# A decode step of attention and MLP on one core: wo's rows per partition, w1 in two transfers, w2's blocks in another order

## The chip, the core and the metric

The kernel runs on one core of a Trainium2 chip. A core has a matrix engine (TensorE, PE in the profile, with its weight loads listed as PEld), a vector engine (VectorE, DVE), a scalar engine for activations (ScalarE, ACT), GpSimd (POOL) and a sequencer that issues transfers (SyncE, SP). Sixteen DMA engines move data between the main memory (HBM) and the on-chip memory SBUF, which has 128 partitions. Matmuls write to another memory, PSUM. The metric is the time of one execution on the device in microseconds, lower is better; several executions are made and the median is given.

## What is computed

One token for each of four sequences (B = 4) goes through one transformer block: an attention over a cache of 4096 positions with 32 heads of 128, and an MLP with 1728 hidden units. The model's width is 640. Everything is bf16 in memory.

```python
def _A_ref(x, k_cache, v_cache, wq, wo):       # x: (4, 1, 640)
    q = (x @ wq).reshape(B, Sq, 32, 128).transpose(0, 2, 1, 3)
    scores = einsum("bhqd,bhkd->bhqk", q, k_cache) * (128 ** -0.5)
    p = softmax(scores)
    o = einsum("bhqk,bhkd->bhqd", p, v_cache)
    return o.transpose(0, 2, 1, 3).reshape(B, Sq, 32 * 128) @ wo

def _B_ref(x, w1, b1, w2):
    h = x @ w1 + b1
    act = h * tanh(log1p(exp(-abs(h))) + where(h > 0, h, 0))
    return act @ w2

h  = x + _A_ref(layernorm(x), k_cache, v_cache, wq, wo)
h2 = h + _B_ref(layernorm(h), w1, b1, w2)
```

The two caches are 134 MB each. wq and wo are 5.2 MB each, w1 and w2 2.2 MB each.

## The kernel before

**Work units.** The caches are cut into NG = 32 groups: group g is one sequence b = g % 4 and one set hq = g // 4 of four heads (G = 4). A K block of a group has the tile `kt`, [128, R = 128, 128]: a head takes 32 partitions, and a partition holds 128 positions in a row, 32 KB. V is held in the same way in `vt`. There are two buffers for each of them (KBUFS, VBUFS), and one transfer of 4096 KB loads one block. The last K block comes in two transfers, the last V block in four (L95 to L98).

**A group's steps** (loop from L408). `mul_and_sum` (L339) multiplies a K block in place by the broadcast q on DVE (L348), in four pieces, and PE sums the products over the head dimension with matmuls against the identity (L355). `finish_sum` (L364) reduces the rest on DVE. `softmax(g - 1)` (L374) finds the maximum by a PE transpose and forms the exponentials on ACT, with their sums. `pv_moving(g - 1)` (L252) multiplies the probabilities with V on PE, `pv_copy` takes the result out of PSUM on ACT, and `add_blocks(g - 2)` (L267) sums it into the o of four sequences. When a set of four groups is done, `row_sums` and `normalise` (L292, L304) divide by the sums of the exponentials and write `otn[:, hq]` in bf16: a partition is one of the 128 head dimensions, and the columns are sequence and head.

**The output projection** `project(hq)` (L325) adds the four heads of a set into the PSUM tile `yT` with 20 matmuls: weights are 128 x 128 pieces of `wo_sb`, the moving side is `otn` with four columns. It runs after `pv_moving` of the steps in `PROJ_AT` (L224): g = 14 to 17 for sets 0 to 3, g = 22, 26, 30 for sets 4 to 6. The last set is projected behind the loop (L499).

**Order of instructions.** The program is written out by hand (L75): each engine runs its instructions in the order of the code, and semaphores hold one back until its operands are there. All loads but x's are issued by SP in code order: at the end of step g, K block g + 2, then V block g + 1, then (steps 8 to 11, `WO_AT`) a quarter of wo, eight heads (L447). In step 8 the 3.4 KB row b1 follows (L452). The transfers of SP's queue are carried out in this order too, by all 16 DMA engines, and an issue waits on SP until its buffer is free.

**wo's layout.** `A_wo.rearrange("(h p) n -> p h n", p=128)`: partition p of head h holds row 128 h + p, so each row of 640 elements is a piece of 1280 bytes.

**Weights of the MLP** (L468 to L480). w1 and the large blocks of w2 share the tile `w12`, which takes the place of a K buffer. w1 is one transfer of 2160 KB with rows of 3456 bytes (five chunks of 128 rows, DC = 5). w2 has 1536 rows in three large blocks (CK = 3) with four rows to a partition (5120 bytes in a piece), then `w2s_sb` (128 rows) and `w2r_sb` (the last 64 rows). Transfers are issued in the order w1, w2s, w2r, w2's large blocks.

**The tail** (L486 to L620). After the last V part: `pv_stationary` (L280), normalise, project the last set, add the residual (hT, L505), the layernorm's mean by a matmul (L513), `h2T` (L520), the squares (L527). Then 70 matmuls form `h1_ps` (L534): 14 chunks c of the hidden units (FC = 14; the chunk C2 = 13 has 64), for each the five chunks dc of the width. After c = 4 the variance's matmul is put in, and ACT loads the table for Exp (L547). The activation takes seven operations on DVE and ACT (L550 to L581). 70 more matmuls form `y2T` (L596), in the order w2s, w2r, large blocks. Residual, transpose and one transfer out end the kernel.

Of the kernel before, what the change touches and what calls it, by code (L numbers as in the profile page):

```python
# [8 lines left out]
FP32 = mybir.dt.float32  # L9
BF16 = mybir.dt.bfloat16  # L10
ACT = mybir.ActivationFunctionType
# [5 lines left out]
def kernel(  # L17
# [24 lines left out]
    nc = tc.nc  # L42

    B, Sq, D = A_x.shape
    _, H, Sk, Dh = A_k_cache.shape
    F = B_w1.shape[1]
    N = B * Sq
    DC = D // 128
    G = 4
    PH = 128 // G  # L50
# [4 lines left out]
    HQ = H // G  # L55
# [4 lines left out]
    WOC = 8  # L60
# [7 lines left out]
    CI = 4  # L68
    CK = F // (128 * CI)
    FM = CK * CI * 128  # L70
    C2 = F // 128
    FREM = F - C2 * 128
    FC = C2 + 1

    ctx.enter_context(tc.manual_schedule())  # L75

# [6 lines left out]
    consts = ctx.enter_context(tc.tile_pool(name="consts", bufs=1))  # L83
# [34 lines left out]
    ident = consts.tile([128, 128], BF16)  # L118
# [7 lines left out]
    eps_t = consts.tile([128, 1], FP32)  # L126
# [9 lines left out]
    nc.gpsimd.memset(rs2[:, :, :], 0.0)  # L136
    b1T = consts.tile([128, FC], FP32)
    nc.gpsimd.memset(b1T[:, :], 0.0)
    otn = consts.tile([128, HQ, N, G], BF16)

    for q in range(G):
        nc.vector.tensor_copy(
            out=sel[:, :, q, q * PH : (q + 1) * PH],
            in_=ident[0:N, 0:N].unsqueeze(2).to_broadcast([N, N, PH]),
# [27 lines left out]
    ps = ps_cm.__enter__()  # L172
# [51 lines left out]
    PROJ_AT = {B1_AT + 1 + hq: hq for hq in range(4)}  # L224
    PROJ_AT.update({4 * (hq + 1) + 2: hq for hq in range(4, HQ - 1)})
    for hq in Q_AT[-1]:
# [12 lines left out]
        out=pick[:, :],  # L239
        in_=ident_f[:, :].rearrange("p (t i) -> p i t", t=T)[:, 0 : J * G, :],  # L240
# [63 lines left out]
    def normalise(hq):  # L304
        nc.vector.tensor_tensor(
            out=otn[:, hq, :, :],
            in0=ot.pop(hq)[:, :, :],
            in1=rls.pop(hq)[:, :, :],
            op=ALU.mult,
        )  # L310
# [3 lines left out]
    def f_chunk(rows, c):  # L314

        if c < CK * CI:
            k, i = divmod(c, CI)
            block = rows[:, k * 128 * CI : (k + 1) * 128 * CI]
            return block.rearrange("p (f i) -> p i f", i=CI)[:, i, :], 128
        return rows[:, c * 128 : min(F, (c + 1) * 128)], min(F - c * 128, 128)  # L320

    yT = ps.tile([128, DC, N], FP32, tag="yT")
    wo_sb = []

    def project(hq):  # L325

        for h in range(hq * G, (hq + 1) * G):
            for c in range(DC):
                nc.tensor.matmul(
                    yT[:, c, :],  # L330
                    lhsT=wo_sb[0][:, h, c * 128 : (c + 1) * 128],
                    rhs=otn[:, hq, :, h % G],
                    start=(h == 0 and c == 0),
                    stop=(h == H - 1 and c == DC - 1),
                )
# [72 lines left out]
    for g in range(NG):  # L408
        hq, b = divmod(g, N)
        for part in range(NP):  # L410
            now = mul_and_sum(g, part)
            before = None
            next(now)
            if part > 0:
                finish_sum(g, part - 1)
                if g >= 2:
                    add_blocks(g - 2)
                    if b == 1:
                        row_sums(hq - 1)
                        normalise(hq - 1)  # L420
            elif g >= 1:
                finish_sum(g - 1, NP - 1)
                before = softmax(g - 1)
                next(before)
            next(now)
            if before is not None:
                next(before)
        kts.pop(g)
        if g + 2 < NG:
            kts[g + 2] = load_k(g + 2)  # L430
        if 1 <= g < NG - 1:
            pv_moving(g - 1, 0, R)
            pv_copy(g - 1)
            vts.pop(g - 1)
        if g in PROJ_AT:
            project(PROJ_AT[g])
        if g + 1 < NG:
            vts[g + 1] = load_v(g + 1)
        for n in Q_AT.get(g, ()):
            q_chunk(n)  # L440
            q_broadcast(n)
        if g in WO_AT:

            if not wo_sb:
                wo_sb.append(wbig.tile([128, H, D], BF16, tag="w", name="wo_sb"))
            h0 = WO_AT[g] * WOC
            nc.sync.dma_start(  # L447
                out=wo_sb[0][:, h0 : h0 + WOC, :],
                in_=A_wo.rearrange("(h p) n -> p h n", p=128)[:, h0 : h0 + WOC, :],
            )  # L450
            if WO_AT[g] == 0:
                nc.sync.dma_start(out=b1_row[:, :], in_=B_b1.rearrange("(o f) -> o f", o=1))  # L452
        if g == B1_AT:
            b_ps = ps.tile([128, FC], FP32, tag="small", name="b_ps")
            for c in range(FC):
                cols, fw = f_chunk(b1_row[:, :], c)
                nc.tensor.matmul(
                    b_ps[0:fw, c : c + 1],
                    lhsT=cols,
                    rhs=ident[0:1, 0:1],  # L460
                    start=True,
                    stop=True,
                )
            nc.vector.tensor_copy(out=b1T[:, 0:C2], in_=b_ps[:, 0:C2])
            nc.vector.tensor_copy(out=b1T[0:FREM, C2:FC], in_=b_ps[0:FREM, C2:FC])


    mlp = ctx.enter_context(tc.tile_pool(name="mlp", bufs=1))  # L468
    w12 = kpool.tile([128, DC * F + CK * CI * D], BF16, tag="kt", name="w12")
    w1_sb = w12[:, 0 : DC * F].rearrange("p (c f) -> p c f", c=DC)  # L470
    w2_sb = w12[:, DC * F :].rearrange("p (k i n) -> p k i n", k=CK, i=CI)
    w2s_sb = mlp.tile([128, D], BF16)
    w2r_sb = mlp.tile([FREM, D], BF16)

    w2_view = B_w2[0:FM, :].rearrange("(k p i) n -> p k i n", k=CK, i=CI)
    nc.sync.dma_start(out=w1_sb, in_=B_w1.rearrange("(c p) n -> p c n", p=128))
    nc.sync.dma_start(out=w2s_sb[:, :], in_=B_w2[FM : C2 * 128, :])
    nc.sync.dma_start(out=w2r_sb[:, :], in_=B_w2[C2 * 128 : F, :])
    for k in range(CK):
        nc.sync.dma_start(out=w2_sb[:, k], in_=w2_view[:, k])  # L480

    h1_ps = ps.tile([128, FC, N], FP32, tag="qq", name="h1_ps")
    nc.vector.memset(h1_ps[FREM:128, FC - 1, :], 0.0)

# [15 lines left out]
    dummy = consts.tile([N, 1], FP32)  # L500
# [6 lines left out]
    def column_means(src, name):  # L507
        part = mlp.tile([128, N], FP32, name=f"{name}_part")
        nc.vector.tensor_reduce(
            out=part[:, :], in_=src[:, :, :].rearrange("p c n -> p n c"), axis=AX.X, op=ALU.add  # L510
        )
        m_ps = ps.tile([128, N], FP32, tag="small", name=f"{name}_ps")
        nc.tensor.matmul(m_ps[:, :], lhsT=mean_f[:, :], rhs=part[:, :], start=True, stop=True)  # L513
        return m_ps

    m_ps = column_means(hT, "mean")
    h2T = mlp.tile([128, DC, N], BF16)
    hc = mlp.tile([128, DC, N], FP32)
    for dst in (h2T, hc):
        nc.vector.tensor_tensor(  # L520
            out=dst[:, :, :],
# [4 lines left out]
    sq = mlp.tile([128, DC, N], FP32)  # L526
# [1 line left out]


    rstd = mlp.tile([128, N], FP32)  # L530
    for c in range(FC):
        fw = f_chunk(w1_sb[:, 0, :], c)[1]
        for dc in range(DC):
            nc.tensor.matmul(  # L534
                h1_ps[0:fw, c, :],
                lhsT=f_chunk(w1_sb[:, dc, :], c)[0],
                rhs=h2T[:, dc, :],
                start=(dc == 0),
                stop=(dc == DC - 1),
            )  # L540
        if c == 4:
            v_ps = column_means(sq, "var")
            std = mlp.tile([128, N], FP32)
            nc.scalar.activation(
                out=std[:, :], in_=v_ps[:, :], func=ACT.Sqrt, bias=eps_t[:, :], scale=1.0
            )
            nc.scalar.activation(out=dummy[:, :], in_=eps_t[0:N, :], func=ACT.Exp)  # L547
            nc.vector.reciprocal(out=rstd[:, :], in_=std[:, :])
    h1n = mlp.tile([128, FC, N], FP32)
    nc.vector.tensor_tensor(  # L550
        out=h1n[:, :, :],
# [6 lines left out]
        out=h1s[:, :, :],  # L558
# [9 lines left out]
        out=tb[:, :, :],  # L568
# [8 lines left out]
        out=ta[:, :, :], in0=tb[:, :, :], scalar1=-0.5, scalar2=-1.0, op0=ALU.mult, op1=ALU.add  # L577
# [4 lines left out]
        out=act_t[:, :, :],  # L582
# [5 lines left out]
    )  # L588

    y2T = ps.tile([128, DC, N], FP32, tag="ot", name="y2T")  # L590
    w2_of = [(w2s_sb[:, :], CK * CI), (w2r_sb[:, :], C2)]
    w2_of += [(w2_sb[:, c // CI, c % CI, :], c) for c in range(CK * CI)]
    for i, (w2, c) in enumerate(w2_of):
        rows = 128 if c < C2 else FREM
        for dc in range(DC):
            nc.tensor.matmul(  # L596
                y2T[:, dc, :],
                lhsT=w2[:, dc * 128 : (dc + 1) * 128],
                rhs=act_t[0:rows, c, :],
                start=(i == 0 and dc == 0),  # L600
                stop=(i == FC - 1 and dc == DC - 1),
# [3 lines left out]
        out=oT[:, :, :].rearrange("p n c -> p c n"),  # L605
# [7 lines left out]
        lhsT=oT[:, :, :].rearrange("p n c -> p (n c)"),  # L613
        rhs=ident[:, :],
        start=True,
        stop=True,
# [35 lines left out]
```

## Time and profile before

| What | us |
|---|---|
| median of three executions | 670.66 |
| lowest and highest of them | 670.47, 671.0 |
| the profiled execution, its own time | 670.71 |
| its span, first to last instruction | 668.9 |

Busy time in the profiled execution, from the first part of the page:

| Engine | busy us | share of the span |
|---|---|---|
| PE | 440.6 | 66% |
| PEld | 200.7 | 30% |
| DVE | 353.0 | 53% |
| ACT | 113.8 | 17% |
| POOL | 2.4 | 0% |

The page counts 15478 packets of the DMA engines with 283.80 MB, 424 GB/s over the span; 5591 of the packets are under 2 KB. Its row of the DMA engines' busy share, in 40 slices of the span, is 9 (90% or more) in all slices but the last. "Landing" is the time from the issue of a transfer to the moment when its completion is seen. In the timeline a row begins with the start and the length in us; a "q" behind an engine's name is its sequencer; brackets hold the idle time before the row and what ended it. TensorE's granted clock was 0.838 of full speed over the span and 0.50 from 655 us on.

### The profile page before, as it was taken

The numbers are of one execution on the slowest core, as the hardware profiler recorded it, in microseconds if no ns is written. First come the engines' busy times: TensorE is split into PE (matmuls) and PEld (weight loads), VectorE is DVE, ScalarE is ACT, GpSimd is POOL, SyncE is SP. The second block draws the span as 40 slices with busy tenths as digits, with TensorE's granted clock in tenths as the row PEclk, the third lists the DMA queues.
The fourth block names the chain that finished last, engine by engine and source line by source line (L and its number), as shares of the span: only waits on it lengthen the run. The fifth ranks groups of instructions, "written<-read, shape, count | busy, mean of one in ns | idle before, by whom it ended". The sixth has DMA issues, their size and how long they took to land.

```text
span 668.9 us, 6865 instructions
## 1 busy us (share of the span) xinstructions
PE 440.6 (66%) x2969; PEld 200.7 (30%) x2969; DVE 353.0 (53%) x306; ACT 113.8 (17%) x345; POOL 2.4 (0%) x13
## 2 busy tenths in 40 slices
PE   0588777887667475367666857757555875667775
PEld 0233333343222232133222323323222332223335
DVE  2486445556655356236654545657454566545732
ACT  0022122131111111011110111111011121111131
POOL 1000000000000000000000000000000000000000
PEclk9997889797777886797777789778788797788985
DMA  9999999999999999999999999999999999999995
GB/s 375 437 436 435 424 429 437 434 434 427 430 437 432 427 422 418 443 423 434 431 428 433 434 436 430 427 433 436 434 431 428 435 434 435 436 426 426 436 415 211
DMA packets 15478, 283.80 MB, mean 424 GB/s; under 512 B 1299, under 2 KB 5591, under 8 KB 6616
## 3 DMA queue, kind: packets, MB, share of 16 engines
q1 hardware_dynamic: 15440, 283.36, 98.8%
q8 instruction: 23, 0.38, 0.2%
q14 instruction: 7, 0.06, 0.0%
q10 hardware_dynamic: 8, 0.01, 0.0%
HBM read 283.35 MB, written 0.01 MB: 424 GB/s over the span
## 4 chain that ended last, share of the span: by engine, by line
DMA 63%; DVE 17%; PE 17%; issue 1%; SPq 0%; ACT 0%; DVEq 0%
DMA kt<-in_A_k_cache_dram 59%; DVE kt L348 15%; PE s L355 14%; DMA w<-in_B_w_dram 4%; DVE s_sb L367 2%; PE tr L380 1%; PE p_ps L255 1%; PE h_ps L534 0%; DVE mx L385 0%; PE q_ps L193 0%; PE tr L393 0%; PE y2T L596 0%; PE qb_ps L207 0%; SPq L98 0%; ACT q_all L200 0%
## 5 line engine op out<-in xcount | busy, mean ns | idle before, releaser
L355 PE MATMUL s<-kt,ident 128*128 128x512 bf16 x1024 | 296.8, 442 | 196.3 <-DVE kt L348 193.1
L348 DVE TENSOR_TENSOR kt<-kt,qbs 128x4096 bf16<-128x4096 bf16 x128 | 291.5, 2279 | 240.1 <-DMA kt<-in_A_k_cache_dram 240.1
L355 PEld LDWEIGHTS <-ident 128*128 128x128 bf16 x1024 | 110.1, 111 | 342.2 <-issue 170.6
L398 ACT ACTIVATE e<-s_sb,nbs 32x128 bf16<-32x128 f32 x128 | 74.0, 578 | 2.5
L255 PE MATMUL p_ps<-vt,e 128*16 128x512 bf16 x1016 | 64.5, 397 | 1.2 <-DMA vt<-in_A_v_cache_dram 1.2
L395 ACT COPY nbs<-tr 128x4 f32<-128x4 f32 x32 | 5.2, 162 | 331.2 <-PE tr L393 331.2
L265 ACT COPY p_sb<-p_ps 128x512 f32<-128x512 f32 x32 | 18.8, 586 | 159.7 <-PE p_ps L255 159.7
L367 DVE TENSOR_REDUCE s_sb<-s 128x64 f32<-128x512 f32 x64 | 43.5, 680 | 3.8 <-PE s L355 3.8
L271 PEld LDWEIGHTS ot<-pick,p_sb 128*128 128x128 f32 x256 | 34.3, 196 | 6.2 <-ACT p_sb L265 1.9
L255 PEld LDWEIGHTS <-e 128*16 128x16 bf16 x1016 | 23.1, 91 | 40.2 <-issue 20.0
L398 ACT ACTIVATION_READ_ACCUMULATOR e<-s_sb,nbs 32x1 f32 x128 | 32.2, 252 | 0.0
L271 PE MATMUL ot<-pick,p_sb 128*128 128x4 f32 x256 | 31.4, 246 | 0.9 <-ACT p_sb L265 0.7
L385 DVE TENSOR_REDUCE mx<-tr 1x4 f32<-1x128 f32 x32 | 8.9, 278 | 24.3 <-PE tr L380 24.3
L193 PE MATMUL q_ps<-wq_sb,xT 128*4 128x512 bf16 x40 | 11.0, 409 | 9.8 <-DMA wq_sb<-in_A_wq_dram 9.8
L380 PE MATMUL tr<-ident_f,pm 128*1 128x128 f32 x64 | 15.6, 335 | 1.2 <-DVE pm L378 1.2
L393 PEld LDWEIGHTS tr<-mx,nscale 1*128 1x128 f32 x64 | 9.4, 182 | 13.8 <-issue 12.3
L302 DVE RECIPROCAL rl<-l_ps 128x16 f32<-128x16 f32 x8 | 2.1, 258 | 21.0 <-PE l_ps L294 21.0
L207 PE MATMUL qb_ps<-q_all,sel 4*128 4x128 bf16 x128 | 9.2, 225 | 5.3 <-ACT q_all L200 5.3
L393 PE MATMUL tr<-mx,nscale 1*128 1x4 f32 x64 | 12.2, 258 | 0.4 <-DVE mx L385 0.4
L207 PEld LDWEIGHTS <-sel 4*128 4x128 bf16 x128 | 8.4, 98 | 9.1 <-issue 9.1
L200 ACT CAST q_all<-q_ps 4x512 bf16<-4x512 f32 x8 | 4.6, 575 | 35.0 <-PE q_ps L193 35.0
L380 PEld LDWEIGHTS tr<-ident_f,pm 128*1 128x1 f32 x64 | 2.8, 81 | 23.3 <-issue 23.3
(81 smaller groups left out, 69.5 us busy)
## 6 DMA issues: line engine op xcount, KB each, us to landing
kt<-in_A_k_cache_dram SPq DMA_DIRECT2D x31, 4096.0 KB, 25.2
vt<-in_A_v_cache_dram SPq DMA_DIRECT2D x31, 4096.0 KB, 32.8
wq_sb<-in_A_wq_dram SPq DMA_DIRECT2D x1, 5120.0 KB
wo_sb<-in_A_wo_dram SPq DMA_DIRECT2D x4, 1280.0 KB, 30.1
kt<-in_A_k_cache_dram SPq DMA_DIRECT2D x2, 2048.0 KB, 17.5
vt<-in_A_v_cache_dram SPq DMA_DIRECT2D x4, 1024.0 KB, 20.1
w<-in_B_w_dram SPq DMA_DIRECT2D x1, 2160.0 KB, 28.3
w<-in_B_w_dram SPq DMA_DIRECT2D x3, 640.0 KB, 16.0
```

The lines of the kernel that those rows point to most:

```text
L193: nc.tensor.matmul(q_ps[:, :], lhsT=xT[:, c, :], rhs=wq_sb[:, c, n * QC : (n + 1) * QC], start=(c == 0), stop=(c == DC - 1),)
L207: nc.tensor.matmul(qb_ps[:, b * Dh : (b + 1) * Dh], lhsT=sel[:, b, q, :], rhs=q_all[:, h * Dh : (h + 1) * Dh], start=(q == 0), stop=(q == ...
L255: nc.tensor.matmul(p_ps[c0 : c0 + J * G, :], lhsT=e2[g % NE2][:, r : r + J, :].rearrange("p j q -> p (j q)"), rhs=vts[g][:, r : r + J, :]. ...
L265: nc.scalar.copy(out=blocks[g][:, :], in_=p_ps[:, :])
L271: nc.tensor.matmul(o, lhsT=p_sb[:, j * Dh : (j + 1) * Dh], rhs=pick[:, j * G : (j + 1) * G], start=(j == 0), stop=(stop and j == J - 1),)
L348: nc.vector.tensor_tensor(out=kt[:, :, d0 : d0 + DQ], in0=kt[:, :, d0 : d0 + DQ], in1=qbs[:, hq, b, d0 : d0 + DQ].unsqueeze(1).to_broadcas ...
L355: nc.tensor.matmul(s_ps[:, :, :], lhsT=ident[:, :], rhs=kt[:, :, d : d + W], start=(d == 0), stop=(d == Dh - W),)
L367: nc.vector.tensor_reduce(out=s_sbs[g][:, part * RP : (part + 1) * RP], in_=s_of.pop((g, part))[:, :, :], axis=AX.X, op=ALU.add,)
L380: nc.tensor.matmul(tr_ps[0:1, 0:128], lhsT=pm[:, :], rhs=ident_f[:, :], start=True, stop=True)
L385: nc.vector.tensor_reduce(out=mx[:, :], in_=tr_ps[0:1, 0:128].rearrange("o (a b) -> o a b", a=G), axis=AX.X, op=ALU.max,)
L393: nc.tensor.matmul(nb_ps, lhsT=nscale[:, :], rhs=mx[:, :], start=True, stop=True)
L398: nc.scalar.activation(out=e2[g % NE2][p0:p1, :, q], in_=s_sb[p0:p1, :], func=ACT.Exp, bias=nb[p0:p1, q : q + 1], scale=SCALE, accum_out=r ...
```

## The change

- wo: the seven first sets of four heads are loaded with four consecutive rows of wo to a partition, that is partition p of a set holds rows 4 p to 4 p + 3 of its 512. Each set is a transfer of its own, so a step issues two in place of one. The last set keeps its layout.
- The o of a set is rearranged to match: `regroup(hq)` has 16 matmuls whose weights are 32 columns of the identity (every fourth one) and one copy on ACT into `o4`. It is called in the steps of `PROJ_AT`, between the two pieces of the second half of the K block. `project` reads `o4` for these sets.
- w1 is loaded in two transfers, chunks 0 to 2 and chunks 3 to 4 of its rows; the matmuls of h1 run in two passes over all 14 chunks of hidden units, and each pass needs one of the transfers. The order of the chunks is 0, 13, 1 to 12. PSUM accumulates over both passes.
- w2's large blocks are issued right after w1, then w2r and w2s; `y2T` takes them in the same order.

```diff
+    W1_PARTS = ((0, 3), (3, DC))
...
+    o4 = consts.tile([128, HQ - 1, G, N], BF16)
+    ident4 = ident[:, :].rearrange("p (j i) -> p i j", i=G)
+
+    def regroup(hq):
+        o4_ps = ps.tile([128, G, N], FP32, tag="small", name=f"o4_{hq}")
+        for q in range(G):
+            for i in range(G):
+                nc.tensor.matmul(
+                    o4_ps[q * PH : (q + 1) * PH, i, :],
+                    lhsT=ident4[:, i, :],
+                    rhs=otn[:, hq, :, q],
+                    start=True,
+                    stop=True,
+                )
+        nc.scalar.copy(out=o4[:, hq, :, :], in_=o4_ps[:, :, :])
...
-                    rhs=otn[:, hq, :, h % G],
+                    rhs=o4[:, hq, h % G, :] if hq < HQ - 1 else otn[:, hq, :, h % G],
...
+                if g in PROJ_AT:
+                    regroup(PROJ_AT[g])
...
-            nc.sync.dma_start(
-                out=wo_sb[0][:, h0 : h0 + WOC, :],
-                in_=A_wo.rearrange("(h p) n -> p h n", p=128)[:, h0 : h0 + WOC, :],
-            )
+            for h in range(h0, h0 + WOC, G):
+
+                order = "(p i) n -> p i n" if h + G < H else "(i p) n -> p i n"
+                nc.sync.dma_start(
+                    out=wo_sb[0][:, h : h + G, :],
+                    in_=A_wo[h * Dh : (h + G) * Dh, :].rearrange(order, i=G),
+                )
...
-    nc.sync.dma_start(out=w1_sb, in_=B_w1.rearrange("(c p) n -> p c n", p=128))
-    nc.sync.dma_start(out=w2s_sb[:, :], in_=B_w2[FM : C2 * 128, :])
-    nc.sync.dma_start(out=w2r_sb[:, :], in_=B_w2[C2 * 128 : F, :])
+    w1_view = B_w1.rearrange("(c p) n -> p c n", p=128)
+    for c0, c1 in W1_PARTS:
+        nc.sync.dma_start(out=w1_sb[:, c0:c1], in_=w1_view[:, c0:c1])
     for k in range(CK):
         nc.sync.dma_start(out=w2_sb[:, k], in_=w2_view[:, k])
+
+    nc.sync.dma_start(out=w2r_sb[:, :], in_=B_w2[C2 * 128 : F, :])
+    nc.sync.dma_start(out=w2s_sb[:, :], in_=B_w2[FM : C2 * 128, :])
...
-    for c in range(FC):
-        fw = f_chunk(w1_sb[:, 0, :], c)[1]
-        for dc in range(DC):
-            nc.tensor.matmul(
-                h1_ps[0:fw, c, :],
-                lhsT=f_chunk(w1_sb[:, dc, :], c)[0],
-                rhs=h2T[:, dc, :],
-                start=(dc == 0),
-                stop=(dc == DC - 1),
-            )
-        if c == 4:
...
+    for c0, c1 in W1_PARTS:
+        for c in (0, C2, *range(1, C2)):
+            fw = f_chunk(w1_sb[:, 0, :], c)[1]
+            for dc in range(c0, c1):
+                nc.tensor.matmul(
+                    h1_ps[0:fw, c, :],
+                    lhsT=f_chunk(w1_sb[:, dc, :], c)[0],
+                    rhs=h2T[:, dc, :],
+                    start=(dc == 0 and c == 0),
+                    stop=(dc == DC - 1 and c == C2 - 1),
+                )
+            if c0 == 0 and c == 4:
...
-    w2_of = [(w2s_sb[:, :], CK * CI), (w2r_sb[:, :], C2)]
-    w2_of += [(w2_sb[:, c // CI, c % CI, :], c) for c in range(CK * CI)]
+    w2_of = [(w2_sb[:, c // CI, c % CI, :], c) for c in range(CK * CI)]
+    w2_of += [(w2r_sb[:, :], C2), (w2s_sb[:, :], CK * CI)]
```

More of the change, by code (lines that the diff above doesn't have):

```diff
@@ L530 @@
     rstd = mlp.tile([128, N], FP32)
-    for c in range(FC):
-        fw = f_chunk(w1_sb[:, 0, :], c)[1]
-        for dc in range(DC):
-            nc.tensor.matmul(
-                h1_ps[0:fw, c, :],
-                lhsT=f_chunk(w1_sb[:, dc, :], c)[0],
-                rhs=h2T[:, dc, :],
-                start=(dc == 0),
-                stop=(dc == DC - 1),
-            )
-        if c == 4:
[L542 to L548, printed above, removed]
+    for c0, c1 in W1_PARTS:
[10 more added lines that the diff above has]
+            if c0 == 0 and c == 4:
+                v_ps = column_means(sq, "var")
+                std = mlp.tile([128, N], FP32)
+                nc.scalar.activation(
+                    out=std[:, :], in_=v_ps[:, :], func=ACT.Sqrt, bias=eps_t[:, :], scale=1.0
+                )
+                nc.scalar.activation(out=dummy[:, :], in_=eps_t[0:N, :], func=ACT.Exp)
+                nc.vector.reciprocal(out=rstd[:, :], in_=std[:, :])
     h1n = mlp.tile([128, FC, N], FP32)
```

## The prediction

> **What bounds the kernel.** I read the page's transfer part and its chain first, then the windows, the issue lists and the last 20 us of the timeline. Transfers and chain on the page:
>
> ```profile
> q1 hardware_dynamic: 15440, 283.36, 98.8%
> q8 instruction: 23, 0.38, 0.2%
> DMA 63%; DVE 17%; PE 17%; issue 1%; SPq 0%; ACT 0%; DVEq 0%
> ```
>
> The sixteen DMA engines carry packets of the SP queue during 98.8% of the span, so the kernel lasts as long as its transfers, plus a start and a tail. DVE and PE on the chain are the work between two waits for kt. A K block lands some 25 us after its issue (page, part 6), while 4 MB at the 433 GB/s of the window from 300 to 600 us take 4.194 / 0.433 = 9.7 us: about 15 us of other traffic are always queued in front of it, and an issue that comes a few us late costs nothing.
>
> So two things count: how long the DMA queue is, and what follows its last landings. First wo, by when it is issued (start, length) and how long it takes to land, behind the V block just in front of it in the queue:
>
> ```profile
> 215.63 0.38 SPq L98 DMA_DIRECT2D vt<-in_A_v_cache_dram  x1
> 216.06 2.02 SPq L447 DMA_DIRECT2D wo_sb<-in_A_wo_dram  x1
> ```
> ```profile
> vt<-in_A_v_cache_dram SPq DMA_DIRECT2D x1, 4096.0 KB, 27.2
> wo_sb<-in_A_wo_dram SPq DMA_DIRECT2D x1, 1280.0 KB, 30.1
> ```
>
> V lands at 215.63 + 27.2 = 242.83, wo at 216.06 + 30.1 = 246.16: wo holds the queue for 3.33 us. The first and third wo transfers give 3.27 and 3.25 in the same way; the mean is 3.28 us for 64 packets of 1280 bytes on each DMA engine, 51 ns a packet. At 433 GB/s the 1.31 MB would take 3.03.
>
> Packets of 5120 bytes exist in w2's large blocks. Issues, and what they needed to land:
>
> ```profile
> 644.97 0.86 SPq L480 DMA_DIRECT2D w<-in_B_w_dram  x1
> 645.87 3.63 SPq L480 DMA_DIRECT2D w<-in_B_w_dram  x1
> ```
> ```profile
> w<-in_B_w_dram SPq DMA_DIRECT2D x1, 640.0 KB, 15.7
> w<-in_B_w_dram SPq DMA_DIRECT2D x1, 640.0 KB, 16.3
> ```
>
> They land at 660.67 and 662.17: 1.50 us for 8 packets on each engine, 187 ns each. The third has no landing in the list; by the same step it lands at 663.67.
>
> The tail, in the timeline (start, length, engine, in brackets the idle time before it and what ended it):
>
> ```profile
> 650.30 1.01 PE L255 MATMUL p_ps<-vt,e 128*16 128x512 bf16 x8 [1.15 <-DMA vt<-in_A_v_cache_dram]
> 656.81 0.17 DVE L520 TENSOR_TENSOR h2T<-hT,mean_ps 128x20 bf16<-128x20 f32 x1 [0.68 <-PE mean_ps L513]
> 657.32 0.19 DVE L509 TENSOR_REDUCE var_part<-sq 128x4 f32<-128x20 f32 x1
> 658.42 0.96 PE L534 MATMUL h_ps<-h2T,w 128*128 128x4 bf16 x25 [1.65 <-DMA w<-in_B_w_dram]
> 659.24 0.57 PE L513 MATMUL var_ps<-var_part,mean_f 128*128 128x4 f32 x2
> 659.67 1.76 PE L534 MATMUL h_ps<-h2T,w 128*128 128x4 bf16 x45
> 660.13 1.28 ACT L547 ACT_TABLE_LOAD   x1
> 661.47 0.22 DVE L550 TENSOR_TENSOR h1n<-h_ps,rstd 128x56 f32<-128x56 f32 x1 [1.14 <-PE h_ps L534]
> 663.53 0.27 PE L596 MATMUL y2T<-act_t,w2s_sb 128*128 128x4 bf16 x5 [2.11 <-DVE act_t L581]
> 663.96 1.76 PE L596 MATMUL y2T<-act_t,w 128*128 128x4 bf16 x60
> ```
>
> The reader sees two transfers that end a wait here: a V part at 650.30 and w1 at 658.41. h2T was ready at 656.98, so PE waited 658.41 - 656.98 = 1.43 us for w1 alone. w2's matmuls run without a gap: its last block landed some 1.4 us before its turn (about 665.1).
>
> **wo, part by part.** Seven of eight groups of four heads change from 4 packets of 1280 bytes to one of 5120 per partition: per DMA engine 224 packets become 56. By w2's row 16 such packets take 16 x 0.187 = 2.99 us in place of 3.28, 0.29 per 1280 KB, and 3.5 times that is 1.0. By the 433 GB/s it is 3.5 x 0.25 = 0.88. The trace's records of single packets give 55 ns (1280 bytes) and 196 (5120, median): 56 x (4 x 55 - 196) = 1.34, the upper end. A lower end comes from w1: it lands at 658.41 behind the last V part (issued 629.63, landing 23.1 later, 652.73), 5.68 us for 40 packets of 3456 bytes, 389 GB/s; at that rate 1280 KB would take 3.37 and the change lose 3.5 x 0.09 = 0.3. I take 0.9, because packet size and alignment match w2's.
>
> In the Trainium skill, "DMA: Bandwidth & Descriptors", the section "Specifications" asks for at least 512 bytes for line rate, so 1280 would already be enough and wo's saving nothing; the sum would be the tail's 1.43 alone. The row of 51 ns against 187 for four times the bytes says otherwise, by 8%.
>
> More transfers: wo goes from four issues to eight, w1 from one to two. SP gains five issues of about 0.43 us (2.2 us), spread over stages in which it waits 406.6 us in all for DVE before a K load; the 15 us of queued traffic cover it, and uncovered it would cost these 2.2. What a cut transfer costs the DMA engines is seen in the last V block: its four parts of 1024 KB land between 645.41 (628.31 + 17.1) and 652.73, three steps of 2.44, so 9.76 for the block against 9.7 whole: 0.01 per cut, nothing. The same skill page ("Anatomy of one DMA") fits a fixed 2.0 us to each transfer on GpSimd's path; an estimate by it, added for five more transfers, would be 10 us and a slower kernel. The V parts show no such step when transfers stand in a queue.
>
> **Regrouping o.** Seven times 16 matmuls of 4 columns and one ACT copy. Such matmuls run in the tail at 0.96 / 25 = 38 ns, so 0.6 us, and 0.16 us for a copy of this size (nbs, L395): some 5.5 us in all. It is issued on PE between the matmuls of the second half block, while DVE multiplies for 2.28 us; the projection that needs o4 comes after the whole PV of that step, 1.9 us later. In the one step where otn is fresh (g = 17, after normalise) PE waits for two DVE operations (0.26 and 0.17 us, L302 and L305) that stand ahead of the next multiply. Behind PE's wait stand the score matmuls of the same half, which wait for that multiply anyway. Even 1 us lost per step only eats idle time before the next K block (DVE idles 3.88 us before the block at 628.38); I cost it at nothing, 5.5 with the cover gone. PE then has 224 more instructions; 5938 went with 23 instruction packets, 258 each, so one more packet comes. It holds one of 16 engines for 0.2% x 16 x 668.9 / 23 = 0.93 us: nothing if it falls on an engine that isn't last, 0.93 if it does. I take 0.1. The queue is thus shorter by s = 0.9 - 0.1 = 0.8, and kt, vt and all that follows comes 0.8 earlier.
>
> **w1 in two passes.** The first transfer has 24 of 40 packets per engine; it lands 16 x 0.142 = 2.27 before the second, at 656.14 by the old clock, and the first pass waits for h2T (656.98) instead. 42 matmuls and the var matmul: 42 x 0.039 + 0.3 = 1.94, to 658.92; the second part is there at 658.41, before its turn. So h1 starts 1.43 earlier and runs through. The var matmul comes after 18 of them, 0.7 us in; var_part is ready 0.53 after h2T. The table load ends 0.8 before Exp is wanted, as before. What is late next is the chain from the V part at 650.30, and that moves by s alone.
>
> **w2's order.** The large blocks no longer wait for 12 small packets (12 x 0.051 = 0.6 us): the last lands at 663.07, needed after 40 of the y2T matmuls, which begin at 663.53 - 1.43 = 662.10, so at 663.3. The small ones land at 663.67, needed at 664.1. The cover is only 0.2 and 0.4 us: worth nothing by itself, but in the old order the last large block would be due after 50 matmuls, at 663.6, and land at 663.67. s moves all of this alike.
>
> **Sum:** 1.43 + 0.8 = 2.2 us. The profiled execution took 670.71 (span 668.9, 1.8 around it), 0.05 over the median of 670.66; I subtract from the median: 668.5.
>
> **Rivals.**
> 1. Forecast: 668.5; with s from 0.3 to 1.34 it runs from 667.8 to 669.0. Chance 0.62.
> 2. wo saves nothing (w1's rate, or the instruction packet on the last engine takes it back): s between -0.3 and 0.3, about 669.2. For it: w1's 3456-byte packets are no faster per byte than wo's. Against: w2's rows. 0.18.
> 3. w2's landings take the place of w1's: one engine 0.93 later than the rest leaves the last block 0.6 late: 669.1. For it: the thin cover, and 147 GB/s in the window 660 to 664, where only some engines still work. 0.07.
> 4. The change doesn't do what it says: the first pass waits for both parts, as they lie in one tile (w12). Then s alone is left: 669.9. Against: PE already waits for single parts of vt. 0.06.
> 5. Slower: four rows read in one piece are slow for wo. To give back the tail's 1.43 and lose 1.34 more, the 56 packets must cost 2.8 us extra: 51 x 4 + 50 = 254 ns each; from there it decides, and gives 672.0 or more. For it: a twentieth of the 5120-byte records are at 262. Against: their median, 196. 0.07.
>
> A measurement of this kernel tells 0.2% (1.34 us) from no change. Faster by more: nearly all of 1, over half of 2, most of 3: 0.77. Within: 4 and the rest: 0.16. Slower: 0.07. The range runs from 667.7 to 669.6, from wo's best packet price to the low end of rival 2.
>
> **What would show it.** In the profile after: 3584 fewer small packets (those under 2 KB from 5591 to about 2007); wo's pieces landing 1.5 us apart; kt's last block about 0.8 earlier than 628.38; h1's first matmul right behind h2T with no wait for w, its second pass without a gap; y2T starting near 661.3 and running without a wait for w2. A wait for w ahead of the first pass speaks for 4, one inside y2T for 3, an unmoved kt for 2, a later one for 5.

## The result, and the profile after

The median went from 670.7 us (eight runs, 670.45 to 671.21) to 668.7 (eight runs, 668.49 to 668.91): 2.0 us less. The ratio is 0.9971, with a 95% interval from 0.9963 to 0.9979. The span of the profiled execution went from 668.9 to 666.8.

The lines of the page after the change that count packets:

```profile
DMA packets 12871, 283.81 MB, mean 426 GB/s; under 512 B 1379, under 2 KB 2087, under 8 KB 4008
q1 hardware_dynamic: 12832, 283.36, 98.9%
q8 instruction: 24, 0.39, 0.2%
```

Packets under 2 KB fell from 5591 to 2087, 80 fewer than the 3584 that wo gave up: packets under 512 bytes rose by 80 (1299 to 1379), 16 for each of the five transfers more. The DMA engines are as busy as before (98.9%), so the queue is still what bounds the loop, and it got shorter. There is one more instruction packet.

How much shorter is seen at the last K block. First the row of the timeline before, then that of the timeline after (start, length, engine, idle time in front and its end):

```profile
628.38 2.29 DVE L348 TENSOR_TENSOR kt<-kt,qbs 128x4096 bf16<-128x4096 bf16 x1 [3.88 <-DMA kt<-in_A_k_cache_dram]
```
```profile
627.50 2.29 DVE L367 TENSOR_TENSOR kt<-kt,qbs 128x4096 bf16<-128x4096 bf16 x1 [3.49 <-DMA kt<-in_A_k_cache_dram]
```

0.88 us earlier in this pair of executions, and DVE still sits idle 3.49 us before it: what PE and ACT do more for the regrouping (the last one has its matmuls at 623.88 and its copy at 624.30) ended before this block came. The 0.88 has some spread: in all nine traces of kernels that load wo as the changed kernel does, this row begins between 627.32 and 627.61; in the two traces with the old wo at 628.38 and 628.08. So the block comes 0.5 to 1.1 us earlier, 0.7 in the mean. The issue and the landings of the last two wo pieces after the change:

```profile
249.14 0.90 SPq L471 DMA_DIRECT2D wo_sb<-in_A_wo_dram  x2
```
```profile
wo_sb<-in_A_wo_dram SPq DMA_DIRECT2D x1, 640.0 KB, 41.2
wo_sb<-in_A_wo_dram SPq DMA_DIRECT2D x1, 640.0 KB, 42.3
```

The first lands at 249.14 + 41.2 = 290.3. The second was issued about 0.47 later (half of the 0.90 and the gap between the two) and landed at 291.9, about 1.5 us behind. This second piece is the one that kept its 1280-byte packets; two sets with 5120-byte packets land as far apart (1.4 us in this profile, 1.5 in a second one of the same kernel). A landing is that of the last of 16 engines and does not tell the two packet sizes apart.

The trace's records of single packets do. They name no engine, but a packet starts where another one ended, and so they can be sorted into 16 chains (the sorting is inferred). Between the short packets that close a transfer, a chain needs 3.32 us for 64 packets of 1280 bytes before (51.9 ns each), 1.66 us for 32 of them in wo's last set after (51.9 ns each again), and 1.55 us for 8 packets of 5120 bytes (193.6 ns each), everywhere within a few ns. So cutting a transfer in two does not shorten it, and larger packets do: 1.66 - 1.55 = 0.11 us for a set, 0.79 for seven.

The tail after the change, in the timeline:

```profile
649.43 1.03 PE L257 MATMUL p_ps<-vt,e 128*16 128x512 bf16 x8 [1.38 <-DMA vt<-in_A_v_cache_dram]
655.96 0.17 DVE L547 TENSOR_TENSOR h2T<-hT,mean_ps 128x20 bf16<-128x20 f32 x1 [0.68 <-PE mean_ps L540]
656.19 0.98 PE L563 MATMUL h_ps<-h2T,w 128*128 128x4 bf16 x18 [0.26 <-DVE h2T L547]
657.02 0.57 PE L540 MATMUL var_ps<-var_part,mean_f 128*128 128x4 f32 x2
657.45 2.03 PE L563 MATMUL h_ps<-h2T,w 128*128 128x4 bf16 x52
659.51 0.22 DVE L579 TENSOR_TENSOR h1n<-h_ps,rstd 128x56 f32<-128x56 f32 x1 [1.41 <-PE h_ps L563]
661.58 1.74 PE L625 MATMUL y2T<-act_t,w 128*128 128x4 bf16 x60 [2.10 <-DVE act_t L610]
663.48 0.29 PE L625 MATMUL y2T<-act_t,w2s_sb 128*128 128x4 bf16 x5
```

The V part in the first row is the third of four; it comes 0.87 earlier, h2T 0.85. The first matmul of h1 now waits for h2T and not for w, and no row of h1 or y2T has a wait for w. h1 begins 658.42 - 656.19 = 2.23 us earlier: 0.85 by the queue, 1.38 by the wait that is gone. But its end gains only 661.43 - 659.48 = 1.95: h1 itself takes 3.29 us where it took 3.01. From there on every row is 1.95 earlier, to the end.

### The profile page after: what moved, and what is told of

Its sections match the earlier page's. It is cut to its first block, busy times and chain, and to the rows that moved or that the text cites. A ratio compares the mean times of both kernels' runs of the same rounds, so it can differ in the third digit from the quotient of the medians.

```text
span 666.8 us, 7101 instructions
## 1 busy us (share of the span) xinstructions
PE 444.7 (67%) x3081; PEld 202.7 (30%) x3081; DVE 353.4 (53%) x306; ACT 115.0 (17%) x352; POOL 2.4 (0%) x13
## 2 busy tenths in 40 slices
DMA packets 12871, 283.81 MB, mean 426 GB/s; under 512 B 1379, under 2 KB 2087, under 8 KB 4008
## 3 DMA queue, kind: packets, MB, share of 16 engines
q1 hardware_dynamic: 12832, 283.36, 98.9%
## 4 chain that ended last, share of the span: by engine, by line
DMA 62%; PE 21%; DVE 15%; issue 1%; ACT 0%; SPq 0%; DVEq 0%; ACTq 0%
DMA kt<-in_A_k_cache_dram 59%; PE s L374 16%; DVE kt L367 13%; DMA vt<-in_A_v_cache_dram 3%; DVE s_sb L386 1%; PE ot L273 1%; PE tr L399 1%; PE p_ps L257 1%; PE h_ps L563 0%; DVE mx L404 0%; PE q_ps L195 0%; PE y2T L625 0%; PE qb_ps L209 0%; PE tr L412 0%; PE o L332 0%
## 5 line engine op out<-in xcount | busy, mean ns | idle before, releaser
L374 PE MATMUL s<-kt,ident 128*128 128x512 bf16 x1024 | 300.0, 446 | 190.1 <-DVE kt L367 187.9
```

What stands on the lines that cost most here:

```text
L374: nc.tensor.matmul(s_ps[:, :, :], lhsT=ident[:, :], rhs=kt[:, :, d : d + W], start=(d == 0), stop=(d == Dh - W),)
```

## The experiments

Each kernel was timed in five rounds beside the kernel before on the same chip; kernels with the same median of before ran together.

| Kernel | median us | before, same call | ratio, 95% interval |
|---|---|---|---|
| wo alone | 669.77 | 670.51 | 0.9988, 0.9979 to 0.9997 |
| tail alone | 669.45 | 670.51 | 0.9984, 0.9976 to 0.9993 |
| changed, w2 in the old order | 668.57 | 670.51 | 0.9971, 0.9961 to 0.9982 |
| changed, w1 in one transfer | 669.74 | 670.51 | 0.9989, 0.998 to 0.9998 |
| changed, narrow chunk once | 668.54 | 670.48 | 0.9971, 0.9959 to 0.9982 |
| changed, regrouping four times | 669.95 | 670.48 | 0.9991, 0.9983 to 1.0 |
| changed, regrouping three times | 669.32 | 670.54 | 0.9981, 0.9972 to 0.999 |
| changed, 21 extra regroupings spread | 669.88 | 670.54 | 0.9991, 0.9982 to 1.0 |
| changed, wo's last set late | 667.97 | 670.48 | 0.9963, 0.995 to 0.9975 |
| the same with three w1 parts | 667.98 | 670.48 | 0.9963, 0.9949 to 0.9977 |
| the changed kernel again | 668.68 | 670.54 | 0.9971, 0.9961 to 0.9982 |
| wo's last set late, again | 668.02 | 670.54 | 0.9963, 0.9951 to 0.9976 |

### The two halves by themselves

The first kernel keeps the wo part of the diff and takes w1, h1 and w2 from before. The second does the reverse; against the changed kernel its edit is this:

```diff
-                    rhs=o4[:, hq, h % G, :] if hq < HQ - 1 else otn[:, hq, :, h % G],
+                    rhs=otn[:, hq, :, h % G],
...
-                if g in PROJ_AT:
-                    regroup(PROJ_AT[g])
...
-            for h in range(h0, h0 + WOC, G):
...
+            nc.sync.dma_start(
+                out=wo_sb[0][:, h0 : h0 + WOC, :],
+                in_=A_wo.rearrange("(h p) n -> p h n", p=128)[:, h0 : h0 + WOC, :],
+            )
```

> The change's wo part alone (four rows to a partition, regroup); w1, h1 and w2 as before. Theory (two separate gains: wo's larger packets shorten the DMA queue by 0.88 us, seen at the last K block; the two passes of h1 take away the wait for w1): kt's last block still lands 0.9 earlier than 628.38, PE still waits about 1.4 us for w1 behind h2T, and the time is 669.8 (0.8 to 1.0 below before). Rival A (all of the gain is made in the tail, the earlier K block only moves a wait): 670.5 or more. Rival B (the shorter queue carries nearly all of it, since w1 then lands early too): 669.0 or less.

> The change's tail alone (w1 in two transfers, h1 in two passes, w2's new order); wo loaded as before, no regroup. Theory: kt's last block lands where it did before (628.4), h2T is ready near 657.0, h1 begins right behind it, and the gain is the 1.43 us of the old wait less 0.28 us by which h1 itself grew (3.01 to 3.29 us): 669.5. Rival A: 668.9 or less (the tail carries it all). Rival B: 670.3 or more (without the shorter queue w1's second part or w2 comes late and takes the gain back).

With wo alone, the timeline has the K block and the wait for w1:

```profile
627.61 2.29 DVE L367 TENSOR_TENSOR kt<-kt,qbs 128x4096 bf16<-128x4096 bf16 x1 [3.89 <-DMA kt<-in_A_k_cache_dram]
657.66 0.98 PE L559 MATMUL h_ps<-h2T,w 128*128 128x4 bf16 x25 [1.63 <-DMA w<-in_B_w_dram]
```

With the tail alone:

```profile
628.08 2.29 DVE L367 TENSOR_TENSOR kt<-kt,qbs 128x4096 bf16<-128x4096 bf16 x1 [3.89 <-DMA kt<-in_A_k_cache_dram]
657.12 0.98 PE L558 MATMUL h_ps<-h2T,w 128*128 128x4 bf16 x18 [0.27 <-DVE h2T L542]
```

wo alone moves the K block (0.77) and leaves the wait; the tail alone removes the wait and moves the K block by 0.30 only, which by code it should not move at all: that is how far two executions differ here. The gains of 0.74 and 1.06 us, each with an interval of some 0.6 us to either side, add up to 1.80, against 1.9 to 2.0 for both. They are separate, and neither rival of these two runs holds.

A rival for wo's part is that SP was held up before: its issue of the row b1 took 20.05 us there (last section). But in the stretch from 187 to 300 us the DMA engines were busy for 1.01 of the time before and 1.00 after (packets overlap a little, so the share can pass 1), so no transfer was missing from the queue, and the 0.79 us of the packet records leave little for it to explain.

### w1 in one transfer

```diff
-    for c0, c1 in W1_PARTS:
+    for c0, c1 in ((0, DC),):
         nc.sync.dma_start(out=w1_sb[:, c0:c1], in_=w1_view[:, c0:c1])
```

> The changed kernel with w1 in one transfer; the matmuls of h1 still in two passes. Theory: the first pass waits for all of w1, which lands at 657.1 (where the second part landed) to 657.5 (w1's own 5.6 us of before), so h1 starts 0.95 to 1.3 us later than 656.19: 669.6 to 670.0. Rival (the gain is from the new order of matmuls or a faster w1 and not from the first pass starting early): 668.7.

```profile
657.31 1.00 PE L563 MATMUL h_ps<-h2T,w 128*128 128x4 bf16 x18 [1.25 <-DMA w<-in_B_w_dram]
```

This row of its timeline shows the wait back, at 657.31, and the time is 669.74, 1.04 above the changed kernel. So of the tail's edits it is the early first transfer that pays, together with the pass that can use it.

### w2's order

```diff
-    for k in range(CK):
-        nc.sync.dma_start(out=w2_sb[:, k], in_=w2_view[:, k])
-    nc.sync.dma_start(out=w2r_sb[:, :], in_=B_w2[C2 * 128 : F, :])
     nc.sync.dma_start(out=w2s_sb[:, :], in_=B_w2[FM : C2 * 128, :])
+    nc.sync.dma_start(out=w2r_sb[:, :], in_=B_w2[C2 * 128 : F, :])
+    for k in range(CK):
+        nc.sync.dma_start(out=w2_sb[:, k], in_=w2_view[:, k])
...
-    w2_of += [(w2r_sb[:, :], C2), (w2s_sb[:, :], CK * CI)]
+    w2_of = [(w2s_sb[:, :], CK * CI), (w2r_sb[:, :], C2)] + w2_of
```

> The changed kernel with w2's old order (small blocks first, in the transfers and in the matmuls). Theory: the last large block lands 0.6 us later, near 662.6, and is wanted after 50 of the y2T matmuls, near 663.1: no wait, 668.7 within 0.2. Rival (w2's order carries part of the gain): y2T has a wait for w in it, 669.1 or more.

The time is 668.57 against 668.70: no difference that this measurement can tell. Its profiled execution is nevertheless instructive. Three rows of its timeline:

```profile
651.12 1.05 PE L273 MATMUL ot<-pick,p_sb 128*128 128x4 f32 x8 [0.74 <-ACT p_sb L267]
657.72 1.29 PE L562 MATMUL h_ps<-h2T,w 128*128 128x4 bf16 x28 [0.33 <-DMA w<-in_B_w_dram]
663.01 0.69 PE L624 MATMUL y2T<-act_t,w 128*128 128x4 bf16 x20 [0.25 <-DMA w<-in_B_w_dram]
```

and the first of them in the changed kernel:

```profile
651.20 1.87 PE L273 MATMUL ot<-pick,p_sb 128*128 128x4 f32 x8 [0.74 <-ACT p_sb L267]
```

The same eight f32 matmuls take 1.05 or 1.87 us: the granted clock in the window from 651 to 653 us was 1.00 in the one execution and 0.50 in the other. With the faster clock h2T begins 0.96 earlier (655.00 against 655.96), and then both w1's second part and w2 are late: PE waits 0.33 in h1's second pass and 0.25 inside y2T. Of the 0.96, 0.47 is left behind h1 (h1n at 659.04 against 659.51) and 0.07 at the transfer out (664.63 against 664.70). So the theory's time came, but its "no wait" did not: a wait inside y2T, the sign named for the rival, did appear. How near the end of the DMA queue lies depends on the clock of that execution; what w2's new order does at the faster clock no run shows.

### Where h1's 0.28 us went

In the trace's single records, matmuls of h1 start every 33 ns or so, but around the chunk of 64 hidden units the steps are 53 to 127 ns. Before, this chunk came last and PE changed the width of its weights once; after, it stands second in both passes. What these steps have over 33 ns adds up to 0.17 us before and 0.47 after: the difference of 0.30 is all of h1's growth.

```diff
-        for c in (0, C2, *range(1, C2)):
+        for c in (*range(FC),) if c0 == 0 else (C2, *range(C2)):
```

> The changed kernel with the narrow chunk (13, 64 hidden units) last in the first pass and first in the second, so that PE changes the width of its weights twice and not four times. Theory (h1 grew from 3.01 to 3.29 us because of these changes of width): h1 takes 3.1 us or less, time 668.5. Rival (h1 grew because PSUM is accumulated in two visits): h1 stays at 3.3 us, time 668.7.

```profile
656.02 0.62 PE L563 MATMUL h_ps<-h2T,w 128*128 128x4 bf16 x15 [0.27 <-DVE h2T L547]
656.63 0.56 PE L540 MATMUL var_ps<-var_part,mean_f 128*128 128x4 f32 x2
657.05 2.18 PE L563 MATMUL h_ps<-h2T,w 128*128 128x4 bf16 x55
```

h1 takes 659.23 - 656.02 = 3.21 us, less than 3.29 but above the 3.1 that was expected; 668.54 us lies 0.15 lower, which five rounds hardly tell. In the single records the steps around the narrow chunk now have 0.28 us over 33 ns, where they had 0.47: the cause is the one that the theory names. That h1 gains only 0.08 has another reason. The var matmul now starts 0.61 us into the pass, behind 15 matmuls that need 15 x 0.033 = 0.49, and the step across it grew from 0.46 to 0.58 us: some 0.1 of the gain is lost there, by the look of it to a wait for var_part, which wasn't tried apart. The Trainium skill ("TensorEngine Tiling (Array Packing)", "Tiling Modes") says that a change of tiling mode drains TensorE; steps of 102 to 127 ns at the changes of width, against 33, agree with it, though that the mode changes here is not seen in the trace.

### What the regrouping costs

A regrouping takes 0.33 us for 16 matmuls and 0.17 for the copy. To see whether that is hidden, it was done four times.

```diff
                 if g in PROJ_AT:
-                    regroup(PROJ_AT[g])
+                    for _ in range(4):
+                        regroup(PROJ_AT[g])
```

> The changed kernel with every regrouping of o done four times over. Each extra one is 0.33 us of PE, 0.17 us of ACT copy and the waits between the two, about 0.9 us in PE's order, 19 us over 21 of them. Theory (hidden before the next K block): 668.7 within 0.3. Rival (PE's work there delays the release of K and V buffers and so the queue): 1 us or more slower, at the full price near 688.

669.95: neither. It is 1.25 us slower than the changed kernel, against a full price of 19. Two rows of its timeline:

```profile
627.49 2.29 DVE L367 TENSOR_TENSOR kt<-kt,qbs 128x4096 bf16<-128x4096 bf16 x1 [3.92 <-DMA kt<-in_A_k_cache_dram]
650.44 1.03 PE L257 MATMUL p_ps<-vt,e 128*16 128x512 bf16 x8 [1.69 <-DMA vt<-in_A_v_cache_dram]
```

The last K block comes when it came with one regrouping (627.50), so PE's work in the loop is hidden, 21 extra times over. What is late, by 1.0 us, is a V part behind it (650.44 against 649.43), and h2T with it (656.98 against 655.96). Without such a delay this V row moves by 0.3 only (649.30 to 649.56 in five traces whose last K block comes at 627.4 to 627.6). The transfers in the stretch from 645.5 to 647 us of this execution have a line that the changed kernel's lack:

```profile
q8 instruction: 1, 0.02, 3.7%
```

It is a packet of 16 KB that brings instructions, on one DMA engine, at 646.0. 672 more PE instructions brought 27 packets in place of 24. Behind it the second of the four V parts lands 3.7 us after the first on the engine that is last, where the step is 2.4 otherwise. Two kernels test this: the same number of instructions in other places (the edit below), and fewer of them (`range(3)` in place of `range(4)` in the edit above).

```diff
                 if g in PROJ_AT:
                     regroup(PROJ_AT[g])
+                else:
+                    for _ in range({7: 2, 8: 2}.get(g, 5 <= g < 30)):
+                        regroup(0)
```

> The changed kernel with 21 extra regroupings of the first set, spread over 19 other steps (two of them have two), so that none has a chain of four. The number of instructions is that of the kernel with four regroupings. Theory (the number of instruction packets and when they come): 27 packets, one near 646, the V part behind it late by about 1.2 us, 669.9 within 0.3. Rival (the chain of four regroupings in one step): 668.7 within 0.2.

> The changed kernel with every regrouping done three times. With four times the last K block landed as in the changed kernel (627.49 against 627.50), but an instruction packet of 16 KB, the 25th, came at 646.0 and the next V part landed 1.2 us late on the last DMA engine. Theory (instruction packets cost, PE's work doesn't): 448 instructions fewer than with four minus the 224 of one, so the 25th packet comes near 657, behind the last V part; only w2 can be late by it: 668.7 to 669.2. Rival (the cost goes by PE's work): two thirds of the 1.25 us, 669.5.

Spread over 19 other steps, the extra work gives 669.88, and in the timeline the same picture:

```profile
627.60 2.29 DVE L367 TENSOR_TENSOR kt<-kt,qbs 128x4096 bf16<-128x4096 bf16 x1 [3.90 <-DMA kt<-in_A_k_cache_dram]
650.79 1.03 PE L257 MATMUL p_ps<-vt,e 128*16 128x512 bf16 x8 [1.42 <-DMA vt<-in_A_v_cache_dram]
```

It too has 27 packets, one at 646.1. With three regroupings (448 PE instructions more than the changed kernel has, 26 packets) the packet comes at 657.5, no V part is late, and w2 is instead:

```profile
663.29 0.69 PE L626 MATMUL y2T<-act_t,w 128*128 128x4 bf16 x20 [0.79 <-DMA w<-in_B_w_dram]
```

669.32 is 0.1 above what the theory gave, since I had reckoned with a wait of some 0.5 there. In size alone it lies nearer the rival's 669.5, but that rival has no place for a wait for w2. So in three traces the last K block comes when it came, and the delay begins right behind an instruction packet, wherever the extra work stands: the cost goes by the packets and by when they come, not by the place of PE's work. Extra instructions without extra work on PE were not tried, so the two are parted by the traces and not by a run of its own. Which DMA engine a packet falls on is inferred from the landings: the records don't name it.

### What bounds the end now

```diff
-            for h in range(h0, h0 + WOC, G):
+            for h in range(h0, min(h0 + WOC, H - G), G):
...
+    nc.sync.dma_start(
+        out=wo_sb[0][:, H - G :, :],
+        in_=A_wo[(H - G) * Dh :, :].rearrange("(i p) n -> p i n", i=G),
+    )
```

> The changed kernel with the last set of wo (640 KB, the one with 1280-byte packets) issued behind the last V block, right ahead of w1, in place of step 11. Theory (what follows the last V part sets the end now, and the DMA queue behind it has only some 1 us to spare): the last K and V blocks land 1.6 us earlier, the first pass of h1 then waits about 0.5 us for w1's first part and y2T comes close to w2's landing at 662.5, so of the 1.6 us some 0.9 is kept: 667.8. Rival A (the end of the DMA queue already binds): 668.6. Rival B (nothing behind V binds): 667.1.

> The kernel with wo's last set behind the last V block, and w1 in three transfers with three passes. Theory (the end of the DMA queue is the next bound): no better than the kernel with two parts, 667.8 within 0.3, with a wait for w inside y2T. Rival (w1's first part is the next bound): 667.4 or less.

(The second has the same edit and `W1_PARTS = ((0, 2), (2, 4), (4, DC))`.) In the timeline of the first:

```profile
654.89 1.00 PE L566 MATMUL h_ps<-h2T,w 128*128 128x4 bf16 x18 [0.81 <-DMA w<-in_B_w_dram]
661.93 0.70 PE L628 MATMUL y2T<-act_t,w 128*128 128x4 bf16 x20 [0.22 <-DMA w<-in_B_w_dram]
```

h2T is ready at 654.29, 1.84 us before the changed kernel's, but both waits for w are back. 667.97 keeps 0.7 of it. Three parts of w1 remove the first wait, and the second takes it up whole:

```profile
661.93 0.69 PE L628 MATMUL y2T<-act_t,w 128*128 128x4 bf16 x20 [0.62 <-DMA w<-in_B_w_dram]
```

With 667.98 nothing is gained: y2T's last 20 matmuls of this tile start at 661.93 in both, when w2's last large block is there. The landing of w2, near the end of the DMA queue, is the bound.

Both kernels ran once more side by side:

> The changed kernel itself, beside the others on the same chip: 668.7.

> The kernel with wo's last set behind the last V block, beside the changed kernel: 0.5 to 0.9 us under it, near 668.0. Rival (its gain came with the other chip's runs): within 0.3 of it.

668.68 and 668.02: wo's last set behind the last V block beats the changed kernel by 0.66 us, and the kernel before by 2.5.

## Why the prediction was right

The forecast was 668.5, and 668.7 was measured. By its steps:

- **wo, 0.9, less 0.1 for the instruction packet.** Right: 0.5 to 1.1 at the last K block, 0.74 for wo alone, 0.79 by the packet records. The mechanism is as stated. That the net 0.8 agrees so closely is in part luck: the steps between landings gave 187 ns for a packet of 5120 bytes and 51 for one of 1280, the records give 193.6 and 51.9. The lower end of the range was a misreading: w1's 5.68 us are the step between two last engines, while a chain of the records needs 5.28 us for the same 40 packets, 132 ns each, so these packets are faster for each byte than wo's and not slower. The upper end, 1.34, took the durations of single packets, which overlap.
- **More transfers at nothing.** Right: with five more the queue was as busy and shorter.
- **The regrouping at nothing.** Right in the loop, shown up to four times. Its parts were mis-sized on the safe side: 0.33 us of PE per set where 0.6 were reckoned.
- **The instruction packet.** 23 became 24, as reckoned from 258 instructions a packet, and did no harm. Its price on the last engine was taken as its own length, 0.93; the landings behind it move by some 1.3 (3.7 against 2.4). The 0.1 that was set aside for the chance of this can't be read off any run.
- **w1's wait, 1.43.** Right in kind, and 1.38 at h1's start. The term that was missed is h1's own length: I carried 39 ns a matmul over to the new order and didn't price the narrow chunk in the middle of each pass. Measured: 0.28 us, most of the difference between 2.2 and 2.0.
- **w2's order at nothing, with a cover of 0.2 and 0.4.** Right: the old order costs no time. The covers were mis-sized. The last large block (issued at 644.54, landing 17.4 us later, 661.9) is there 0.7 before the matmul that wants it, which starts at 662.65. The 0.4 should have been 0.3: y2T's 70 matmuls take 2.19 us, 31 ns each, so the 61st is due at 663.96. The waits for w2 that appear when h2T comes about 1 us earlier fit a cover of 0.7.

The range's ends on the fast side, 667.8 and 667.7, lie a little under what their term gives: 670.66 - 1.43 - 1.34 = 667.9.

Of the rivals, the first pass did start before the second part was there, the 5120-byte packets were not slow, and w2 was waited for only where the chain in front of it was shorter still, or where an instruction packet came between (three regroupings).

## What to carry to other kernels

Where the DMA engines are busy all the time, price a change of layout by what a packet of that size costs in the trace, from packet to packet on one engine rather than from landing to landing, and find the gain again at the last big landing, in more than one execution. A wait for a large transfer at the end of a chain can be removed by cutting transfer and consumer along the same axis; then look at what the new order of the consumer costs by itself. In such a kernel instructions aren't free either: each block of them is a transfer on the same DMA engines.

## What was not expected of the hardware

- In the two kernels with an instruction packet of 16 KB at 646, the V part behind it comes 1.0 and 1.4 us later and the time grows by 1.2; that the packet falls on the DMA engine that is already last is inferred. The Trainium skill ("Runtime: NRT & Kernel Launch", "Instruction fetch mechanics") calls the cost of such a boundary mostly hidden. For PE that holds here (the last K block at 627.49 and 627.60 against 627.50); for data transfers on the same engines the runs with 27 packets show 1.2 us.
- The 16 engines drift apart: the 16 completions of a 4 MB block lie within 1.5 us of each other at the start of the profile before and within 4.9 at the end (the block issued at 614.90). A landing is that of the last one.
- An issue can hold up the issuer for long behind many small packets. The 3.4 KB row b1, issued behind a wo transfer, in the timelines before and after:

```profile
188.26 20.05 SPq L452 DMA_DIRECT2D b_row<-in_B_b_dram  x1
```
```profile
188.87 0.34 SPq L476 DMA_DIRECT2D b_row<-in_B_b_dram  x1
```

With 64 packets per engine right in front, SP stood 20 us in this issue; with two transfers of 8 it took 0.34. The DMA engines stayed busy meanwhile, so it cost no time that the traces show.
- The same eight f32 matmuls behind the third V part took 1.05 us at a granted clock of 1.00 and 1.87 us at 0.50.
